# Causal attention ahead of a mixture of experts: diagonal half blocks of the scores and values as 64x64 matmuls, loads issued from the scores

## The chip, the core and the metric

The kernel runs on one core of one Trainium2 chip. The metric is the device time of one execution in microseconds (us), taken as the median of several runs. In the profile, PE is TensorE (PEld its weight loads), DVE is VectorE, ACT is ScalarE, POOL is GpSimd and SP is SyncE, which issues most of the DMA transfers. A line number such as L904 is a line of the kernel file of that profile.

## The reference

Eight sequences of 576 tokens, eight heads of 64 dimensions, everything in float32. Causal attention is computed with a per-head decay, and its output is the input of a mixture of eight experts in which every token goes to one expert, its own choice or that of the token before it.

```python
scores = scale * np.matmul(q, k.transpose(0, 1, 3, 2))
causal = np.triu(np.ones((S, S), dtype=bool), k=1)
cum = np.cumsum(np.maximum(s, 0.0), axis=-1)
bias = -(cum[:, :, :, None] - cum[:, :, None, :])
scores = np.where(causal, -1000000000.0, scores + np.minimum(bias, 0.0))
...
attn = attn / (np.sum(attn, axis=-1, keepdims=True) + 1e-09)
x = np.matmul(attn, v)                       # then (B, S, H * D)
...
e = fresh_e if s == 0 or local_gate[b, s] < 0.5 else prev_e
h = np.maximum(x[b, s] @ w1[e], 0.0)
out[b, s] = p[e] * (h @ w2[e])
```

## The kernel before

The kernel has two stages that follow each other on TensorE: attention, which also routes the tokens and stores them by expert in a table in HBM, and the experts, which fetch the table's rows and multiply them with the experts' weights (lines L608 and L637). The change lies in the attention stage.

Attention works on "pairs": two heads of one sequence, whose 64 dimensions each fill the two halves of the 128 partitions. There are 32 pairs (`NPAIR`), and the main loop (L1002) takes two of them in each of 16 rounds; a round is called a slot here. The 576 queries are nine blocks of 64 (`NJ`), the keys four chunks of 128 and a last chunk that holds the last 64 keys.

Scores are computed with keys on the output's partitions. `UNITS` says which key chunks and query ranges make one unit: (chunk, first query, last query, place). Four units make a pair, of 384, 384, 448 and 384 columns for each head (`WIDTH`). For a unit, `scores` (L893) takes a PSUM tile of two banks from the rotating pool `ps_s` of three such tiles, runs the matmuls of both heads (64 rows by 128 columns of the array each, the two heads on different rows), lets ScalarE write the exponential into a tile e (L905), and lets GpSimd set to zero what lies past the diagonal (`masked`, L890). A unit can start when the exponential of the unit three before it has emptied its tile. In a chunk that lies on the diagonal, an even query block needs only the first 64 of the 128 keys; the other 64 are computed and then masked.

Values follow when both pairs' eight units are issued: `values` (L924) multiplies, for each query block and each key chunk up to the diagonal, the exponentials (as weights, 128 rows by 64 columns, the two heads side by side) with the values vg, 66 columns wide: 64 dimensions, the key's decay weight, which sums to the denominator, and a one. A pair has 25 block-and-chunk steps for each head. The results lie in two tiles of the pool `ps_o` (blocks 0 to 5 and 6 to 8, `NJA`), each there once, so the second pair's values wait for the first's to be read. VectorE takes the reciprocal and multiplies into the token tile xb (L941, L942).

The values vg come from `weigh` (L876), which multiplies the loaded va with the keys' decay weights on VectorE; `WEIGHED` says up to which pair that is done at the end of each slot. Queries, keys and values come by DMA from SP, in order. A load is held back by a one-element ScalarE copy into its tile (L797, L808) that reads what the load shall follow: the second unit's exponential of the slot's second pair for values of six pairs ahead, and the first pair's outputs for queries and keys of four pairs ahead.

Each engine works in the order in which the program states its instructions[...]. Routing steps are hung into that order with `plan(slot, place, ...)`: places 0 and 1 are behind the first and second pair's scores, 3 and 4 behind their values, 5 at the slot's end. Three slots carry the routing's logits (lp, 160 columns on four 32-column parts of the array, from tiles of `ps_s`), three others the ranks (pos), and the last slot half a logits product; from the seventh slot on GpSimd stores rows of the table (L349).

Of the kernel before, what the change touches and what calls it, by code (L numbers as in the profile page):

```python
# [9 lines left out]
F32 = mybir.dt.float32  # L10
# [26 lines left out]
NJA = 6  # L37
G1 = 2
REF = (127, 415)
UNITS = (((0, 0, 384, 0),), ((0, 384, S, 0), (3, 384, S, 192)), ((1, P, S, 0),), ((2, 256, S, 0), (NF, TS, S, 320)))  # L40
WIDTH = (384, 384, 448, 384)
# [10 lines left out]
FIRST = ((0, P, 0, 3 * P), (P, S, 3 * P, S))  # L52
# [63 lines left out]
class Router:  # L116
# [104 lines left out]
    def logits(self, g, bs=range(GB)):  # L221
        v = self.nc.vector
        st = self.g[g]
        n, groups = self.columns(bs)
        lt = self.s("lt", [P, NJH, 2, WR])
        v.transpose(lt[:, :n].rearrange("p j q e -> p (j q e)"), st.pop("lp"))
        if "l" not in st:
            st["l"] = self.s("l", [P, NC, E + 1])
        l = st["l"]
        for c, (b, j, skip) in enumerate(groups):  # L230
            for r in range(2):
                v.tensor_copy(l[32 * r : 32 * r + 32, b * NJ + j + skip : b * NJ + j + n],
                              lt[32 * c : 32 * c + 32, skip:n, r, : E + 1])
        c = slice(bs[0] * NJ, bs[-1] * NJ + NJ)
        v.tensor_copy(l[DH:, c], l[:DH, c])
# [530 lines left out]
def attention(ctx, tc, q, k, v, s, wx, ident, recs, wend, router, experts):  # L766
# [10 lines left out]
    p_e = pool("p_e", 2)  # L777
    p_x = experts.p_x
# [8 lines left out]
    ins, vs, es, xs, xts = {}, {}, {}, {}, {}  # L787
    heads = [slice(DH * h, DH * h + DH) for h in range(2)]

    def load_qk(n, behind=None):  # L790

        if n >= NPAIR:
            return
        b, hp = divmod(n, HP)
        ins[n] = qb, kb = p_in.tile([P, S], F32, name="qb"), p_in.tile([P, S], F32, name="kb")
        if behind is not None:
            nc.scalar.copy(kb[0:1, 0:1], behind)  # L797
        for k0, k1, q0, q1 in FIRST if n == 0 else ((0, S, 0, S),):
            nc.sync.dma_start(kb[:, k0:k1], k[b][:, hp, k0:k1])  # L799
            nc.sync.dma_start(qb[:, q0:q1], q[b][:, hp, q0:q1])  # L800
# [23 lines left out]
    load_qk(2)  # L824
    load_v(2)
    load_qk(3)
    for n in range(3, NVA):
        load_v(n)
    router.projection(wx)
    wk = once.tile([P, NPAIR, G1 + NB, 2], F32, name="wk")  # L830
    nc.gpsimd.memset(wk[:TL, :, G1 + NF], 0.0)
    for t in vgs:
        nc.gpsimd.memset(t[..., VW - 1 : VW], 1.0)
        nc.gpsimd.memset(t[:TL, G1 + NF, :, VW - 1 : VW], 0.0)
# [19 lines left out]
    def key_weights():  # L854
        cps = banks("cps")[:, 0].rearrange("p (i n) -> p i n", n=B * H)
        i = 0
        for w, n in ((w1, G1), (w2, NB)):
            for c in range(n):
                a = min(c * P, S - P)
                tr(cps[:, i], w[:, a : a + P], ident[: B * H, : B * H])  # L860
                i += 1
        for i in range(G1 + NB):
            d = slice(TL if i == G1 + NF else 0, P)
            nc.vector.tensor_copy(wk[d, :, i, :].rearrange("p n h -> p h n"), cps[d, i].rearrange("p (h n) -> p h n", h=2))
# [24 lines left out]
    def masked(ap, n, base=0):  # L889
        nc.gpsimd.affine_select(out=ap, in_=ap, compare_op=Alu.is_ge, fill=0.0, base=base, pattern=n,  # L890
                                channel_multiplier=-1)

    def scores(n, u):  # L893
        if n >= NPAIR:
            return
        qb, kb = ins[n]
        if u == 0:
            es[n] = [p_e.tile([P, 2, w], F32, name=f"e{i}") for i, w in enumerate(WIDTH)]
        e = es[n][u]
        ps = banks("ps")[:, :, : WIDTH[u]]  # L900
        for c, a, z, at in UNITS[u]:
            key = min(c * P, S - P)
            for h, d in enumerate(heads):
                mm(ps[:, h, at : at + z - a], lhsT=kb[d, key : key + P], rhs=qb[d, a:z], start=True, stop=True)  # L904
        nc.scalar.activation(e, ps, Act.Exp, scale=scale)  # L905
        for c, a, z, at in UNITS[u]:
            m = min(P, z - a)
            if a < c * P + P:
                masked(e[:, :, at : at + m], [[0, 2], [1, m]], P - m)
# [14 lines left out]
    def values(n, j0, j1):  # L924
        b, hp = divmod(n, HP)
        if b not in xs:
            xs[b] = x_tile(b) if b < BX else p_x.tile([P, NJ, 2, XW], F32, name="xb")
        xb = xs[b]
        po = ps_o.tile([P, j1 - j0, VW], F32, name=f"po{j0}")
        for j in range(j0, j1):  # L930
            last = j // 2 if j < NJ - 1 else NF
            for c in range(last + 1):
                for h, d in enumerate(heads):
                    mm(po[d, j - j0, :], lhsT=weights_of(n, c, j, h),  # L934
                       rhs=vgs[n % NV][:, c if j < 2 * G1 else G1 + c, h, :],
                       start=(c == 0), stop=(c == last))

        def evacuate():
            m = j1 - j0
            rec = recs[:, n, j0:j1, :]  # L940
            nc.vector.reciprocal(rec, po[:, :, VW - 2 : VW])  # L941
            nc.vector.tensor_tensor(xb[:, j0:j1, :, 32 * hp : 32 * hp + 32], po[:, :, :DH].rearrange("p j (g i) -> p j g i", g=2),  # L942
                                    rec[:, :, 0].unsqueeze(2).unsqueeze(3).to_broadcast([P, m, 2, 32]), op=Alu.mult)

        return evacuate, po[0:1, 0, 0:1]
# [21 lines left out]
    for g in range(NG - 1):  # L967
        m = HP * GB // 2 * (g + 1)
        plan(m, 1, lambda g=g: router.product(g, of(g), banks))
        plan(m, 3, lambda g=g: router.logits(g))  # L970
        plan(m, 5, lambda g=g: (router.codes(g), router.turn1(g)))
        plan(m + 1, 1, lambda g=g: router.exps(g))
        plan(m + 1, 3, lambda g=g: router.turn2(g))
        plan(m + 2, 1, lambda g=g: router.ranks(g, banks))
        plan(m + 2, 3, lambda g=g: router.rows(g))
        plan(m + 2, 3, lambda g=g: router.gates(g, [xs[b] for b in range(g * GB, g * GB + GB)]))
# [13 lines left out]
    plan(m - 5, 3, lambda: router.assign_early(0))  # L990
# [5 lines left out]
    plan(m - 1, 3, lambda: router.logits(NG - 1, (0,)))  # L996
# [4 lines left out]

    for m in range(NPAIR // 2):  # L1002
        pair = 2 * m, 2 * m + 1
        for n in pair:
            for u in range(len(UNITS)):
                if (n, u) == (0, 2):
                    key_exps()
                scores(n, u)
                if (n, u) == (0, 3):
                    key_weights()  # L1010
                    weigh(0)
                    weigh(1)
                if (n % 2, u) == (1, 1):
                    load_v(n - 1 + NVA, es[n][u][0:1, 0, 0:1])
                    load_v(n + NVA)
            at(m, n - 2 * m)
        for n in pair:
            values(n, 0, NJA)[0]()
            evacuate, done = values(n, NJA, NJ)
            if n % 2 == 0:  # L1020
                load_qk(n + NV, done)
                load_qk(n + 1 + NV)
            evacuate()
            at(m, 3 + n - 2 * m)
# [44 lines left out]
def attention_general(ctx, tc, q, k, v, s, w_gate, w_local, cum_d, x_d, ident, lg):  # L1069
# [24 lines left out]
    def load_batch(b):  # L1094
# [7 lines left out]
        nc.sync.dma_start(kb, k[b])  # L1102
        for hp in range(HP):
            hs = slice(2 * hp, 2 * hp + 2)
            nc.sync.dma_start(vb[:, :, hs], v[b, hp][:, :NF])
            nc.sync.dma_start(vl[:, hs], v[b, hp][TL:, NF])
# [501 lines left out]
```

## Time and profile before

| | |
|---|---|
| Median of 3 runs | 729.83 us (729.41 to 730.94) |
| The profiled execution | 748.85 us, of which the span of its instructions 747.1 us |
| Mean granted TensorE clock in it | 0.994 of full speed |
| PE busy | 729.2 us, 98% of the span, 6537 records |
| PEld, DVE, ACT, POOL busy | 504.9, 257.7, 166.0, 206.7 us |
| Value matmuls (L934) | 3200 records, 105.2 us |
| Score matmuls (L904) | 768 records, 94.7 us |
| Exponentials (L905) | 128, 97.0 us |
| Masks (L890) | 160, 67.2 us |
| HBM traffic | 249 GB/s over the span |

The busy time of an engine is the union of its records. A float32 matmul of the kernel leaves two matmul records, one for each of its two passes, and as many weight loads; two matmuls on different parts of the array run at the same time, so the mean duration of a record says little, and a stage's length is read from the chain of waits or from the order in time. The records of the first expert matmul start 221.6 us into the span; what lies before that is the attention stage.

### The profile page before, as it was taken

To read this page: it belongs to the slowest core of one execution; us is meant where nothing else is said; L and a number is where in the kernel's file an instruction comes from. 1 tells how busy PE (TensorE), PEld (TensorE's weight loads), DVE (VectorE), ACT (ScalarE), POOL (GpSimd) and SP (SyncE) were. 2 spreads that over 40 slices of the span, in tenths; PEclk is the share of its full clock that TensorE was granted. 3 is DMA by queue.
4 is the path that set the end of the run, shared out by engine and by line. 5 is a ranking of instruction groups with operands and counts; after the bars stand their busy time and mean duration, and the time that the engine had idled before them with its cause. 6 is when DMAs were issued, how large, how long until landed. Compare 5 with 4: busy or idle time off the path is not lost.

```text
span 747.1 us, 16231 instructions
## 1 busy us (share of the span) xinstructions
PE 729.2 (98%) x6537; PEld 504.9 (68%) x6537; DVE 257.7 (34%) x714; ACT 166.0 (22%) x355; POOL 206.7 (28%) x453
## 2 busy tenths in 40 slices
PE   8999999999998999999999999999999999999996
PEld 7888878878876567567567365637644676673675
DVE  4656668677756383101100411041132001104110
ACT  4645454354331011011011010201010111110111
POOL 3543367577574245350100011010101001000100
PEclk9999999999998999999999999999999999999999
DMA  8464455665629996598555979996999965976700
GB/s 303 145 189 149 152 191 165 201 199 172 188 81 382 341 396 218 208 424 240 203 190 169 375 258 396 342 382 237 425 334 390 423 215 214 307 268 239 269 15 32
DMA packets 57205, 187.28 MB, mean 251 GB/s; under 512 B 11837, under 2 KB 32061, under 8 KB 49568
## 3 DMA queue, kind: packets, MB, share of 16 engines
q1 hardware_dynamic: 50224, 165.91, 62.3%
q0 software_dynamic: 6800, 20.09, 7.0%
q8 instruction: 53, 0.87, 0.5%
q14 instruction: 32, 0.26, 0.1%
q10 hardware_dynamic: 96, 0.15, 0.1%
HBM read 165.50 MB, written 20.75 MB: 249 GB/s over the span
## 4 chain that ended last, share of the span: by engine, by line
PE 95%; issue 2%; POOL 1%; DVE 1%; DMA 1%; ACT 0%; SPq 0%; POOLq 0%; ACTq 0%
PE yp L637 34%; PE hp L608 31%; PE po L934 13%; PE ps L904 11%; PE hp L599 4%; PE lp L217 2%; DMA qb<-in_q_dram 1%; POOL table L349 0%; ACT e L905 0%; PE pos L301 0%; POOL e L890 0%; PE pos L302 0%; DVE xb L942 0%; SPq L799 0%; POOL out_dram L641 0%
## 5 line engine op out<-in xcount | busy, mean ns | idle before, releaser
L637 PE MATMUL yp<-w2b,hT 128*128 128x512 f32 (+4 forms) x768 | 258.4, 584 | 0.0
L608 PE MATMUL hp<-xT,w1b 128*128 128x256 f32 (+2 forms) x1216 | 232.0, 352 | 0.0
L608 PEld LDWEIGHTS hp<-xT,w1b 128*128 128x128 f32 x1216 | 207.7, 192 | 30.0 <-issue 7.8
L637 PEld LDWEIGHTS yp<-w2b,hT 128*128 128x128 f32 (+3 forms) x768 | 109.9, 167 | 138.4 <-issue 136.1
L641 POOL DMA_INDIRECT out_dram<-y,gi x37 | 36.4, 984 | 412.3 <-DVE y L639 380.0
L610 ACT ACTIVATE hT<-hp 128x256 f32<-128x256 f32 (+2 forms) x152 | 53.6, 353 | 430.4 <-PE hp L608 417.2
L639 DVE TENSOR_SCALAR y<-yp,gi 128x512 f32<-128x512 f32 (+2 forms) x38 | 27.8, 731 | 299.8 <-PE yp L637 293.4
L934 PE MATMUL po<-vg,e 128*64 128x66 f32 x3200 | 105.2, 223 | 6.9 <-issue 5.6
L934 PEld LDWEIGHTS po<-vg,e 128*64 128x64 f32 x3200 | 98.7, 138 | 13.1 <-issue 10.5
L905 ACT ACTIVATE e<-ps 128x768 f32<-128x768 f32 (+1 forms) x128 | 97.0, 837 | 46.5 <-PE ps L904 45.8
L904 PE MATMUL ps<-qb,kb 64*128 64x192 f32 (+4 forms) x768 | 94.7, 398 | 0.6 <-ACT e L905 0.3
L904 PEld LDWEIGHTS ps<-qb,kb 64*128 64x128 f32 x768 | 64.7, 186 | 29.6 <-ACT e L905 14.9
L890 POOL TENSOR_SCALAR_AFFINE_SELECT e<-e 128x256 f32<-128x256 f32 (+1 forms) x160 | 67.2, 444 | 50.3 <-ACT e L905 49.3
L349 POOL DMA_INDIRECT table<-xb,idx x54 | 54.5, 1009 | 19.6 <-issue 16.8
L619 DVE STREAM_TRANSPOSE hT<-hs 32x256 f32<-32x256 f32 x64 | 27.9, 436 | 78.9 <-ACT hs L601 78.1
L884 DVE TENSOR_TENSOR vg<-va,wk 128x256 f32<-128x256 f32 x64 | 41.5, 714 | 0.0
L941 DVE RECIPROCAL recs<-po 128x12 f32<-128x12 f32 x64 | 13.5, 211 | 64.0 <-PE po L934 45.2
L599 PE MATMUL hp<-w1b,xT 128*32 128x512 f32 (+1 forms) x224 | 28.3, 594 | 0.0
L578 DVE STREAM_TRANSPOSE xT<-xq 128x1024 f32<-128x1024 f32 (+1 forms) x23 | 23.6, 1028 | 11.8 <-DMA xq<-table 11.7
L942 DVE TENSOR_TENSOR xb<-po,recs 128x384 f32<-128x384 f32 (+1 forms) x48 | 22.0, 458 | 2.2 <-POOL xb L325 0.6
L599 PEld LDWEIGHTS hp<-w1b,xT 128*32 128x32 f32 (+1 forms) x224 | 8.1, 114 | 17.8 <-issue 17.8
L953 DVE STREAM_TRANSPOSE xt<-xb 128x576 f32<-128x576 f32 x24 | 17.1, 751 | 0.0
(254 smaller groups left out, 202.6 us busy)
## 6 DMA issues: line engine op xcount, KB each, us to landing
w2b<-in_w_dram SPq DMA_DIRECT2D x30, 2048.0 KB
w1b<-in_w_dram SPq DMA_DIRECT2D x29, 2048.0 KB
va<-in_v_dram SPq DMA_DIRECT2D x32, 320.0 KB
kb<-in_k_dram SPq DMA_DIRECT2D x31, 288.0 KB
qb<-in_q_dram SPq DMA_DIRECT2D x31, 288.0 KB
xq<-table SPq DMA_DIRECT2D x56, 130.0 KB
w1b<-in_w_dram SPq DMA_DIRECT2D x4, 512.0 KB
xq<-table SPq DMA_DIRECT2D x20, 65.0 KB
```

The lines of the kernel that those rows point to most:

```text
L349: put = self.nc.gpsimd.indirect_dma_start(out=self.halves, in_=src, element_offset=0, in_offset=None, out_offset=bass.IndirectOffsetOnAxis ...
L599: mm(ps[d, :], lhsT=xT[:, k, d], rhs=self.ws[l][0][:, k, c * 512 : c * 512 + 512], start=(k == 0), stop=(k == DK - 1))
L608: mm(ps[:, :w], lhsT=self.ws[ls[0]][0][:, k, c * P : c * P + P], rhs=xT[:, k, :w], start=(k == 0), stop=(k == DK - 1))
L610: nc.scalar.activation(self.hT[u][:, c, :w], ps[:, :w], Act.Relu)
L619: self.nc.vector.transpose(hT[32 * a : 32 * a + 32, :, 32 * r : 32 * r + 32], hs[32 * r : 32 * r + 32].rearrange("p (c i) -> p c i", i=P)[ ...
L637: mm(ps[d, :], lhsT=hT[:, k, n * P + d.start : n * P + d.stop], rhs=self.ws[l][1][:, k, f : f + w], start=(k == 0), stop=(k == FK - 1))
L641: put = nc.gpsimd.indirect_dma_start(out=self.out[:, :], out_offset=bass.IndirectOffsetOnAxis(ap=gi.bitcast(I32)[:m, n, 0:1], axis=0), in_ ...
L884: nc.vector.tensor_tensor(vg[:, to].rearrange("p c h e -> p (c h) e")[:, :, :DH], va[:, :c].rearrange("p c h e -> p (c h) e"), wk[:, n, to ...
L890: nc.gpsimd.affine_select(out=ap, in_=ap, compare_op=Alu.is_ge, fill=0.0, base=base, pattern=n, channel_multiplier=-1)
L904: mm(ps[:, h, at : at + z - a], lhsT=kb[d, key : key + P], rhs=qb[d, a:z], start=True, stop=True)
L905: nc.scalar.activation(e, ps, Act.Exp, scale=scale)
L934: mm(po[d, j - j0, :], lhsT=weights_of(n, c, j, h), rhs=vgs[n % NV][:, c if j < 2 * G1 else G1 + c, h, :], start=(c == 0), stop=(c == last))
```

## The change

The nine key blocks are stored in another order (`BLOCKS`: 8, 0, 1, 2, 3, 5, 4, 7, 6), so that four chunks of 128 keys hold blocks 0 and 1, 2 and 3, 5 and 4, 7 and 6, and block 8 stands alone in front. The host orders the keys and values so. A unit then contains only whole chunks: for each chunk, the queries from its second block on. Three units make a pair, of 512, 448 and 384 columns. What is left, query blocks 0, 4, 2 and 6 with their own 64 keys, is computed apart: `scores_halves` does this for both pairs of the next slot in 16 matmuls of 64 rows, 64 columns and 64 moving columns, with one exponential and two masks for both pairs; `values_halves` multiplies them with the values, 8 matmuls of 64 rows by 64 columns for each pair. Whole values take 21 steps for each head.

The order of a slot becomes: six score units, half values of the first pair, half scores of the next slot, half values of the second pair, whole values of the first, whole values of the second. The second pair's outputs (pb) lie in a tile of the rotating pool `ps_s` that the score units use too; the first pair's stay in `ps_o`. Output parts are blocks 0 to 3 and 4 to 8.

Loads are held back by the slot's own first exponentials: values of four and five pairs ahead by the first unit of the first pair, queries and keys of four pairs ahead by the third unit of the first pair and the second unit of the second pair, each with its one-element copy. The logits' copies go from VectorE to ScalarE where both sequences are there, and several routing steps move from place 3 to place 1.

```diff
-NJA = 6
+NJA = 4
...
-UNITS = (((0, 0, 384, 0),), ((0, 384, S, 0), (3, 384, S, 192)), ((1, P, S, 0),), ((2, 256, S, 0), (NF, TS, S, 320)))
-WIDTH = (384, 384, 448, 384)
+BLOCKS = (8, 0, 1, 2, 3, 5, 4, 7, 6)
+UNITS = (((0, DH, S, 0),), ((1, 3 * DH, S, DH), (NF, TS, S, 0)), ((2, 5 * DH, S, 0), (3, 7 * DH, S, 256)))
+WIDTH = (512, 448, 384)
...
+HALVES = ((0, 4), (2, 6))
...
-        for k0, k1, q0, q1 in FIRST if n == 0 else ((0, S, 0, S),):
-            nc.sync.dma_start(kb[:, k0:k1], k[b][:, hp, k0:k1])
-            nc.sync.dma_start(qb[:, q0:q1], q[b][:, hp, q0:q1])
+        todo = [(kb, k, 0, S), (qb, q, 0, S)] if n else [(kb, k, 0, DH + P), (qb, q, 0, FIRST), (qb, q, FIRST, S), (kb, k, DH + P, S)]
+        for to, src, a, z in todo:
+            nc.sync.dma_start(to[:, a:z], src[b][:, hp, a:z])
...
-        for c, a, z, at in UNITS[u]:
-            m = min(P, z - a)
-            if a < c * P + P:
-                masked(e[:, :, at : at + m], [[0, 2], [1, m]], P - m)
+        if u == 0:
+            masked(e[:, :, :DH], [[0, 2], [1, DH]], DH)
+        elif u == 1:
+            masked(e[:, :, :P], [[0, 2], [1, P]])
+        else:
+            masked(e[:DH].rearrange("p h (t i) -> p (h t) i", t=2)[:, :, :DH], [[0, 4], [1, DH]])
+
+    def scores_halves(m, ps):
+        if 2 * m >= NPAIR:
+            return
+        eh[m] = p_eh.tile([P, 2, 2, len(HALVES), DH], F32, name="eh")
+        ps = ps[:, :, : 4 * DH]
+        for i in range(2):
+            qb, kb = ins[2 * m + i]
+            for t, blocks in enumerate(HALVES):
+                for side, x in zip(heads, blocks):
+                    at = (2 * i + t) * DH
+                    key = BLOCKS.index(x) * DH
+                    for h, d in enumerate(heads):
+                        mm(ps[side, h, at : at + DH], lhsT=kb[d, key : key + DH], rhs=qb[d, x * DH : x * DH + DH],
+                           start=True, stop=True)
+        nc.scalar.activation(eh[m].rearrange("p h n t i -> p h (n t i)"), ps, Act.Exp, scale=scale)
+        by = eh[m].rearrange("p h n t i -> p (h n t) i")
+        masked(by[:DH], [[0, 8], [1, DH]])
+        masked(by, [[0, 8], [1, DH]], DH)
...
+    def room(n):
+        if n % 2:
+            po = banks("pb")
+            po = [po[:, i] for i in range(2)]
+        else:
+            po = [ps_o.tile([P, 512], F32, name=f"po{i}") for i in range(2)]
...
+    def values_halves(n, po, first):
+        e = eh[n // 2][:, :, n % 2]
+        for t, blocks in enumerate(HALVES):
+            for part, (side, j) in enumerate(zip(heads, blocks)):
+                for h, d in enumerate(heads):
+                    mm(po[part][d, j - PARTS[part][0], :], lhsT=e[side, h, t],
+                       rhs=vgs[n % NV][side, j // 2 + (G1 if part else 0), h, :],
+                       start=(first > 0 and t == 0), stop=(first == 0 and t == 1))
...
-        plan(m, 3, lambda g=g: router.logits(g))
+        plan(m, 1, lambda g=g: router.logits(g))
...
-        plan(m + 1, 3, lambda g=g: router.turn2(g))
+        plan(m + 1, 1, lambda g=g: router.turn2(g))
...
-        plan(m + 2, 3, lambda g=g: router.rows(g))
-        plan(m + 2, 3, lambda g=g: router.gates(g, [xs[b] for b in range(g * GB, g * GB + GB)]))
+        plan(m + 2, 1, lambda g=g: router.rows(g))
+        plan(m + 2, 1, lambda g=g: router.gates(g, [xs[b] for b in range(g * GB, g * GB + GB)]))
...
+    def loads(n, u):
+        step = n % 2, u
+        if (n, u) == (2, 1):
+            load_v(n + NV, es[n][u][0:1, 0, P : P + 1])
+            load_v(n + 1 + NV)
+        elif step == (0, 0):
+            n = n if n > 2 else 0
+            load_v(n + NV, es[n or 2][u][0:1, 0, DH : DH + 1])
+            load_v(n + 1 + NV)
+        elif step == (0, 2):
+            load_qk(n + NV, es[n][u][0:1, 0, DH : DH + 1])
+        elif step == (1, 1):
+            load_qk(n + NV, es[n][u][0:1, 0, P : P + 1])
...
                 scores(n, u)
...
-                if (n % 2, u) == (1, 1):
-                    load_v(n - 1 + NVA, es[n][u][0:1, 0, 0:1])
-                    load_v(n + NVA)
+                if n > 1:
+                    loads(n, u)
             at(m, n - 2 * m)
-        for n in pair:
-            values(n, 0, NJA)[0]()
-            evacuate, done = values(n, NJA, NJ)
-            if n % 2 == 0:
-                load_qk(n + NV, done)
-                load_qk(n + 1 + NV)
-            evacuate()
-            at(m, 3 + n - 2 * m)
+        a, b = pair
+        po = room(a)
...
+        values_halves(a, po, m)
+        halves = banks("ph") if b + 1 < NPAIR else None
+        to = room(b)
+        scores_halves(m + 1, halves)
+        values_halves(b, to, True)
...
+        for i in range(2):
+            if m:
+                values(a, po, i, False, True)
+            evacuate(a, po, i)
+        at(m, 3)
+        for i in range(2):
+            values(b, to, i, False, True)
+            evacuate(b, to, i)
+        at(m, 4)
```

## The prediction

> **What bounds the kernel now.** The page's chain of waits, by engine and line, comes first; then the chain in order of time for two ordinary slots of the attention stage (a slot is one pass of the loop over two head pairs):
>
> ```profile
> PE 95%; issue 2%; POOL 1%; DVE 1%; DMA 1%; ACT 0%; SPq 0%; POOLq 0%; ACTq 0%
> PE yp L637 34%; PE hp L608 31%; PE po L934 13%; PE ps L904 11%; PE hp L599 4%; PE lp L217 2%; DMA qb<-in_q_dram 1%; POOL table L349 0%; ACT e L905 0%; PE pos L301 0%; POOL e L890 0%; PE pos L302 0%; DVE xb L942 0%; SPq L799 0%; POOL out_dram L641 0%
> ```
>
> ```profile
> 55.39 5.76 PE ps L904 x48
> 61.15 2.31 PE lp L217 x64
> 63.46 5.98 PE po L934 x200
> 69.44 5.76 PE ps L904 x48
> 75.20 5.98 PE po L934 x200
> ```
>
> TensorE carries it; the change touches only the attention lines (ps, po). An ordinary slot is 5.76 us of scores and 5.98 us of values, 11.74 us, with no wait of TensorE in the chain. There are 16 slots; three also hold lp (2.31 us), three the two pos matmuls (0.72 us), the last a half lp (1.46 us).
>
> The third view is ScalarE inside one score stage, in order of time. Columns: start, length, engine and line, count.
>
> ```profile
> 71.10 1.61 ACT L905 ACTIVATE e<-ps 128x768 f32<-128x768 f32 x2
> 72.61 1.51 ACT L905 ACTIVATE e<-ps 128x768 f32<-128x768 f32 x2
> 73.30 1.53 ACT L905 ACTIVATE e<-ps 128x768 f32<-128x768 f32 x2
> 74.86 0.19 ACT L808 COPY va<-e 1x1 f32<-1x1 f32 x1
> 74.95 1.59 ACT L905 ACTIVATE e<-ps 128x896 f32<-128x896 f32 x2
> ```
>
> Same trace, narrower windows: exponentials start at 70.39, 71.10, 71.80, 72.61, 73.30, 73.99, 74.95, 75.76. Back to back, one of 768 elements occupies ScalarE 0.69 to 0.71 us and one of 896 0.81 us (71.80 to 72.61), although it finishes 0.1 us later than that. Around the one-element copy the step is 74.95 - 73.99 = 0.96 us: the copy reads the tile just written, so ScalarE runs empty, and it costs 0.28 us (0.27 by these roundings). TensorE ends its unit 0.27 us before the exponential starts (70.12, 70.39). ScalarE is thus almost as full as TensorE here, yet its fifth exponential (73.30) still frees its bank in time.
>
> **The profiled run against the others.** It took 748.85 us (span 747.1), the median is 729.83. The last nine slots, from 93.65 to 221.63 in the chain, took 128.0 us, where clean ones would take 9 x 11.74 + 2 x 2.31 + 1.46 + 2 x 0.72 = 113.2: TensorE shows gaps marked "issue" there. The half lp behind them spans 226.94 to 232.69, 5.75 us instead of 1.46, and the clock granted between 228 and 240 us is 0.72, some 3 us more. Together about 22 us, as much as the difference. So I take the timed runs' slots as clean (11.74 us), cost the change against those, and move the median by the same amount.
>
> **Per-pass prices, same score stage.** A matmul record is one of two passes. 448 columns: 70.77 to 71.15, 0.375 us; four of 192: 0.65 us; so 0.84 ns a column: 512 columns 0.43, 256 0.216, 128 0.109, 64 0.056 us. Two heads' records run at once on two parts of the array. Values: 0.0583 us a pass (5.98/100, less the switch). Leaving scores for values costs 75.13 against 74.93 + 0.06, and a first pass 0.05 longer: 0.20 us; values to scores the same (0.10 before, 0.10 in the first pass).
>
> **The skill.** "TensorEngine Tiling (Array Packing)", Key Properties, says that changing the tiling mode drains TensorE and that tiles run independently; the two 0.20 us switches agree with the first. For the second, lp has four column tiles: 64 records of 160 columns are sixteen groups of 0.134 us, 2.15 us, and 2.31 is measured. A 64x64 mode no run here shows. "TensorE: Matmul & The Clock Gate", LDWEIGHTS, prices a weight load by its columns over 1.2 GHz: 53 ns for 64, just inside a 56 ns pass; agreeing, a 128-column load behind a 64-column pass delays the next by 0.056 us. Its section on measured packing reports sixteen row-and-column tiles at 10.6 times; I lean on that.
>
> **The change, part by part (ordinary slot).**
> *Scores.* Per pair 1,600 columns become 512 + 384 + 64 + 256 + 128 = 1,344: two passes each are 0.86 + 0.644 + 0.112 + 0.432 + 0.218 = 2.27 us against 2.70. Two pairs 4.54, plus 0.11 behind the 64-column passes, plus 0.10 first pass: 4.75.
> *Half scores.* 16 matmuls on four quadrants: 4 groups x 2 passes x 0.056 = 0.45 us. Pairwise it would be 0.90.
> *Half values.* 8 per pair on four quadrants: 4 passes x 0.058 = 0.23 us for each pair.
> *Whole values.* 21 instead of 25 key chunks per pair: 84 passes x 0.0583 = 4.90 against 5.83.
> *Switches.* Three modes a slot instead of two: 0.20 more (bounds 0 and 0.25; I take 0.20, as both present ones).
> TensorE alone: 4.75 + 0.20 + 0.23 + 0.45 + 0.23 + 0.20 + 4.90 + 0.10 = 11.06 us, 0.68 less than now.
> *Banks.* The second pair's outputs leave ps_o and take the three rotating score banks. Counting allocations, half scores take the bank of the fourth exponential, pb that of the fifth; the third unit of the next slot takes pb's, freed about 1 us into that slot by two VectorE reads (0.2 + 0.5 us), needed at 1.8: hidden, with 0.8 us to spare.
> *Loads.* The slot's three copies now sit inside the chain of exponentials: behind the first, third and fifth. The transfers behind them wait on SP for the copy, and are needed a slot later, 12 us or more: hidden. The copies are not. Behind each stand the remaining exponentials, and behind those pb.
> Chain to pb: first exponential 0.96 + 0.27 = 1.23; 1,024 elements 0.92 (768 and 896 extrapolated); copy 0.28; 896 at 0.81; 768 at 0.70; copy 0.28; 0.92; 0.81; finish 0.10: 6.05 us. The current trace restarts a weight load 0.05 us after an exponential ends; with the load, 0.15: pb at 6.2. TensorE gets there at 5.6 (5.8 with a short wait for the second exponential before). Then 0.23 + 0.20 + 4.90 + 0.10: 11.63 us. So 0.57 of the 0.68 us is handed back, and a slot gains 0.11.
> *Masks and the rest.* Five selections a pair (0.3 to 0.4 us each) become three, plus two wide ones for the halves, which are read a slot later: hidden, and values start later than now. Logit copies move from VectorE to ScalarE in three slots, behind the exponentials, ahead of only the half exponential: hidden. Moving rows, gates and turns to an earlier place puts up to 3.5 us of VectorE work ahead of the first pair's evacuation; po is wanted 5 us into the next slot: hidden. Start: first transfers differ by 32 KB.
>
> **The sum.** Eight ordinary slots x -0.11 = -0.9. Three lp slots: lp takes the fourth bank at 5.4 (a 0.25 us wait) and then hides the rest: about 13.9 against 14.06, -0.5 together. Three pos slots shift pb to the sixth exponential, behind the third copy, 7.1: about 12.53 against 12.46, +0.2. Last slot, no half scores: -0.6. First slot, less scoring but two more switches and key weights as now: -0.7 (0 to -1.5). Together -2.5: 727.3 us.
>
> **Rivals.**
> *Full gain.* If the copies cost nothing in the chain, pb is free at 5.64, as TensorE arrives: fifteen slots x -0.68 and the first, -10.5: 719.3. For it: TensorE is 95% of the chain. Against: the measured 0.28 us. It decides once the chain is 0.57 us shorter.
> *Slower: quadrants run two by two.* Halves cost 0.47 + 0.90 + 0.47 instead of 0.91. TensorE reaches pb at 6.5, past ScalarE; the slot is 12.2, +0.45 x 8; lp slots +0.76, pos slots +0.7; about +8.5 in all: 738. For it: no 64x64 record in the trace. Against: lp. It decides where the 1.8 us of halves exceeds about 1.4, the saving less the switch.
> *Starved halves.* 128 instructions (64 records and as many weight loads) in 0.91 us is 140 a us; the densest stretch shown is half lp, 128 in 1.46. At that rate a slot loses 0.17 on top: 730, no change.
>
> **Chances.** Main case 0.52 (own range 725 to 729.5); full gain 0.15; between them, if the new switch is free or the copies overlap partly, 0.06; starved 0.15; two by two 0.12. Faster or slower counts beyond 0.2% (1.5 us), about what a measurement of this kernel can tell from no change. Faster: 0.40 of the main case + 0.15 + 0.05 = 0.60; same: 0.10 + 0.07 = 0.17; slower: the rest, 0.23. For 8 in 10 the range reaches the full gain and part of the slow side: 719 to 734.
>
> **What would show it.** Right: about 11.6 us a slot; a wait of weight loads before the second pair's half values, on an exponential, of about 0.4 us; steps over 1.1 us from a 1,024-element exponential across a copy; 64-column half scores in groups of four within 0.06 us. Wrong: no such wait and slots near 11.1 (full gain); half scores near 0.9 us (pairs); waits on masks or transfers inside a slot; new gaps in the experts' stage, which I hold unchanged.

## The result and the profile after

The changed kernel takes **739.2 us** (median of 6 runs, 733.23 to 742.35), the kernel before 730.41 (729.41 to 731.36) beside it: a ratio of 1.0108 with a 95% interval of 1.0067 to 1.0149, slower where 727.3 was forecast. The profiled execution took 739.1 us, its span is 737.4; the trace below is of this one execution, while the six runs spread over 9 us and those of the kernel before over 2.

The page of the changed kernel, its DMA queues (packets, MB, share of 16 engines) and the chain by engine and line:

```profile
q1 hardware_dynamic: 50224, 165.91, 63.7%
...
q8 instruction: 56, 0.92, 0.5%
...
PE 94%; issue 1%; ACT 1%; DMA 1%; POOL 1%; SPq 0%; DVE 0%; POOLq 0%; ACTq 0%
PE yp L642 35%; PE hp L613 31%; PE ps L915 10%; PE pb L974 6%; PE po L974 5%; PE hp L604 4%; PE lp L221 1%; DMA va<-in_v_dram 1%; ACT e L916 1%; PE ph L937 1%; PE pb L986 1%; PE po L986 1%; SPq L806 0%; POOL table L354 0%; DVE wk L871 0%
```

TensorE still carries it. What went wrong shows only slot by slot, in the chain in order of time of the changed kernel: a clean slot from 32.96 to 44.38, and the next.

```profile
32.96 5.07 PE ps L915 x40
38.03 0.39 PE po L986 x16
38.42 0.47 PE ph L937 x32
38.89 0.44 PE pb L986 x16
39.33 2.60 PE po L974 x84
41.93 2.45 PE pb L974 x84
44.38 5.07 PE ps L915 x40
49.45 0.39 PE po L986 x16
49.84 0.47 PE ph L937 x32
50.30 0.44 PE pb L986 x16
50.74 2.60 PE po L974 x84
53.34 1.33 PE pb L974 x45
54.68 1.69 issue
56.37 1.38 PE pb L974 x39
```

The clean slot is 11.42 us; it was 11.74 before. The second loses 1.85 us in the middle of its last matmuls (from the last matmul's due start to 56.37), and the profile names no engine and no transfer as the releaser: "issue". Such a gap stands in nine further places behind it, and one of 0.8 us ahead of it, at 32.63.

**What the gaps have in common.** I numbered TensorE's records in order of start: its 13,850 weight loads and matmuls and the 117 records of its sequencer, most of them semaphores, between them. The first instruction behind each long gap of this trace has number 192 or 193 above a multiple of 256: 2,241 at 56.37, 4,033 at 95.87, 4,545 at 109.09, 6,336 at 149.75, 6,849 at 163.63. (Without the sequencer's records the pattern is lost: the remainders are then 169, 157, 151, 137 and 131.) Queue q8 of the page carries 56 packets of 16 KB, and TensorE starts about 256 instructions from one packet to the next: I read them as its program, as its 13,967 records make 54.6 packets of 256. Mostly a packet comes 180 to 295 instructions after the last. Ahead of these five gaps it is 384 to 453, and nowhere else in the trace over 376; the packet that is missing at 54.68 moves at 53.99, the one before it at 43.94. At a distance of 256 to 290 instructions it would have moved at 51.1 to 51.6 us, so it is 2.4 to 2.9 us late. I conclude that TensorE has run to the end of its packet and waits for the next one.

The windows of the same trace (us, busy time of TensorE, its weight loads, VectorE, ScalarE, GpSimd; granted clock; DMA share; GB/s) show what the packet competes with, and what a long gap costs besides:

```profile
50.00:52.00 2.00, 2.00 (x82) 1.82 (x74) 0.56 (x2) 1.60 (x4) 1.13 (x3) 1.00 0.96 291
52.00:54.00 2.00, 2.00 (x76) 2.00 (x74) 0.65 (x3) 0.22 (x1) 1.01 (x2) 1.00 1.05 394
54.00:56.00 2.00, 0.68 (x23) 0.54 (x19) 0.68 (x3) 0.00 (x0) 0.00 (x0) 1.00 0.49 184
...
109.00:110.00 1.00, 0.91 (x26) 0.91 (x28) 0.00 (x0) 0.00 (x0) 0.52 (x1) 0.84 0.16 58
110.00:111.00 1.00, 1.00 (x24) 1.00 (x22) 0.00 (x0) 0.00 (x0) 0.00 (x0) 0.50 0.47 150
111.00:112.00 1.00, 1.00 (x16) 0.88 (x14) 0.22 (x1) 0.22 (x1) 0.00 (x0) 0.50 0.03 4
```

From 50 to 54 us the 16 engines are full with the slot's loads, and the packet starts in the burst's last microsecond. After the gaps of 2.28 us (109.09) and 2.88 us (163.63) the granted clock is 0.50 for about 3.4 us each, 1.7 us lost each. "TensorE: Matmul & The Clock Gate", Part 1, names an idle window of about 3.4 us for that; here 2.3 us of idling came before it.

**Two levels of chips.** The runs fell on several chips. The kernel before takes 730 us on some (as in both comparisons above) and 746 on others; the profile of before, at 748.85 us, is of the second kind. Each numbered chip served one group of runs, so that the level belongs to the chip and not to the time of the runs is not shown; "chip of the 746 level" below means no more than what the kernel before took there. Ratios are always against the kernel before on the same chip. For each trace two sums are given: gaps of over 0.2 us between the starts of consecutive matmuls, beyond the first one's two passes, from 40 us to the end of attention (which leaves out a late packet near 32 us that several of the traces have), (a) at a packet's end, numbers 192 and 193, and (b) within 3 us behind the start of a GpSimd table store. The changed kernel's trace above has (a) 11.1 and (b) 0.4; before's has 0.2 and 10.3.

### The profile page after: what moved, and what is told of

It is laid out like the page before. It is cut to its first block, busy times and chain, and to the rows that moved or that the text cites. A ratio compares the mean times of both kernels' runs of the same rounds, so it can differ in the third digit from the quotient of the medians.

```text
span 737.4 us, 16944 instructions
## 1 busy us (share of the span) xinstructions
PE 717.6 (97%) x6925; PEld 493.2 (67%) x6925; DVE 251.4 (34%) x689; ACT 168.5 (23%) x381; POOL 202.7 (27%) x421
## 4 chain that ended last, share of the span: by engine, by line
PE 94%; issue 1%; ACT 1%; DMA 1%; POOL 1%; SPq 0%; DVE 0%; POOLq 0%; ACTq 0%
PE yp L642 35%; PE hp L613 31%; PE ps L915 10%; PE pb L974 6%; PE po L974 5%; PE hp L604 4%; PE lp L221 1%; DMA va<-in_v_dram 1%; ACT e L916 1%; PE ph L937 1%; PE pb L986 1%; PE po L986 1%; SPq L806 0%; POOL table L354 0%; DVE wk L871 0%
## 5 line engine op out<-in xcount | busy, mean ns | idle before, releaser
L916 ACT ACTIVATE e<-ps 128x1024 f32<-128x1024 f32 (+2 forms) x96 | 83.3, 905 | 60.1 <-PE ps L915 55.8
L915 PE MATMUL ps<-qb,kb 64*128 64x64 f32 (+5 forms) x644 | 84.8, 415 | 0.8 <-ACT e L916 0.8
L915 PEld LDWEIGHTS ps<-qb,kb 64*128 64x128 f32 x644 | 53.3, 191 | 30.5 <-ACT e L916 11.2
L899 POOL TENSOR_SCALAR_AFFINE_SELECT e<-e 128x128 f32<-128x128 f32 (+2 forms) x96 | 41.5, 441 | 54.3 <-ACT e L916 53.6
L974 PE MATMUL pb<-vg,e 128*64 128x66 f32 x1344 | 46.7, 228 | 9.8 <-issue 7.5
L974 PEld LDWEIGHTS pb<-vg,e 128*64 128x64 f32 x1344 | 43.9, 143 | 11.2 <-issue 8.8
L974 PE MATMUL po<-vg,e 128*64 128x66 f32 x1344 | 43.2, 223 | 0.3 <-issue 0.3
L974 PEld LDWEIGHTS po<-vg,e 128*64 128x64 f32 x1344 | 40.8, 138 | 1.6 <-issue 0.4
L892 DVE TENSOR_TENSOR vg<-va,wk 128x256 f32<-128x256 f32 x64 | 37.4, 647 | 0.0
L583 DVE STREAM_TRANSPOSE xT<-xq 128x1024 f32<-128x1024 f32 (+1 forms) x23 | 23.6, 1027 | 14.3 <-DMA xq<-table 14.1
L899 POOL TENSOR_SCALAR_AFFINE_SELECT eh<-eh 64x512 f32<-64x512 f32 (+1 forms) x32 | 21.1, 660 | 12.4 <-ACT eh L939 8.9
## 6 DMA issues: line engine op xcount, KB each, us to landing
w2b<-in_w_dram SPq DMA_DIRECT2D x30, 2048.0 KB, 12.5
```

The costliest lines, as they stand in the source:

```text
L892: nc.vector.tensor_tensor(vg[:, to].rearrange("p c h e -> p (c h) e")[:, :, :DH], va[:, :c].rearrange("p c h e -> p (c h) e"), wk[:, n, to ...
L916: nc.scalar.activation(e[:, :, : WIDTH[u]], ps, Act.Exp, scale=scale)
L974: of = mm(po[part][d, j - a, :], lhsT=weights_of(n, c, j, h), rhs=vgs[n % NV][:, c if j < 2 * G1 else G1 + c, h, :], start=(first and i == ...
```

## The experiments

### Where the loads stand

Both kernels with the other's loads, and the changed kernel with half of the loads moved back (chip of the 746 level, before 745.82 us).

`e1_old_loads`: the changed kernel, all loads at before's places.

```diff
-        step = n % 2, u
-        if (n, u) == (2, 1):
...
-        elif step == (0, 2):
-            load_qk(n + NV, es[n][u][0:1, 0, DH : DH + 1])
-        elif step == (1, 1):
-            load_qk(n + NV, es[n][u][0:1, 0, P : P + 1])
+        if (n % 2, u) == (1, 1):
+            load_v(n - 1 + NVA, es[n][u][0:1, 0, P : P + 1])
+            load_v(n + NVA)
...
+            if i:
+                load_qk(a + NV, po[1][0:1, 0, 0:1])
+                load_qk(b + NV)
             evacuate(a, po, i)
```

> The changed kernel with its loads at the places of the kernel before (values six pairs ahead behind the second unit of the second pair, queries and keys behind the first pair's outputs); all matmuls as changed. Theory (TensorE's instruction fetch comes late behind the load transfers, which the change puts under the instruction-rich half and whole values): the issue gaps of 0.5 to 2.9 us in pb vanish or nearly, a slot takes 11.2 us, and the time is 720 to 725 us. Rival A (more instructions, 544 instead of 496 a slot and 128 of them within 1 us, starve TensorE wherever the loads stand): gaps as before, 734 to 740 us. Rival B (the copies within ScalarE's chain cost the time): only 0.2 us a slot, so 3 us less than the changed kernel.

747.71 us, ratio 1.0017 (1.0005 to 1.0029), a miss: 720 to 725 would have been 0.986 to 0.993 of the kernel before. Clean slots of 11.11 us are as expected and most late packets are gone, (a) 2.7; but (b) is 13.9.

`e1_before_new_loads`: the kernel before with `loads` as in the change, behind its own units.

```diff
-                if (n % 2, u) == (1, 1):
-                    load_v(n - 1 + NVA, es[n][u][0:1, 0, 0:1])
-                    load_v(n + NVA)
+                if n > 1:
+                    loads(n, u)
...
-            if n % 2 == 0:
-                load_qk(n + NV, done)
-                load_qk(n + 1 + NV)
```

> The kernel before with its loads let go as the change does it (values behind the first unit of the first pair, queries and keys behind the last unit of the first pair and the third of the second); all matmuls as before. Theory (late instruction fetch): issue gaps of about 1 us in several slots, 735 to 745 us. Rival A (the denser instruction stream): no new gaps, 730 to 733 us, the copies in the chain of exponentials alone adding up to 0.2 us a slot.

748.86 us, 1.0039 (1.0023 to 1.0056). Score stages of 6.14 instead of 5.76 us: the copies in the chain of exponentials cost 0.38 us a slot. (a) 0.5, (b) 9.7: with before's matmuls the loads' new place makes hardly a packet late. The gaps of about 1 us in several slots that the theory expected here did not come, so a burst of loads alone is not enough either.

`e1_old_qk`: the changed kernel, only queries and keys at the old place.

```diff
-        elif step == (0, 2):
-            load_qk(n + NV, es[n][u][0:1, 0, DH : DH + 1])
-        elif step == (1, 1):
-            load_qk(n + NV, es[n][u][0:1, 0, P : P + 1])
...
+            if i:
+                load_qk(a + NV, po[1][0:1, 0, 0:1])
+                load_qk(b + NV)
             evacuate(a, po, i)
```

> The changed kernel with only the loads of queries and keys at the place of the kernel before; values' loads as changed. Theory: these four transfers of a slot (1.15 MB) make most of the burst under the values, so most of the loss goes: 722 to 728 us. Rival A: 734 to 740 us.

744.35 us, **0.9974** (0.9959 to 0.9989): faster than before by 0.26%, at the edge of what was expected (722 to 728 would have been 0.989 to 0.997). Clean slots of 11.21 us, (a) 0.6, (b) 15.7.

`e1_old_v`: only the values' loads at the old place, so that all of a slot's loads come closely behind each other.

```diff
...
-        elif step == (0, 2):
+        if step == (1, 1):
+            load_v(n - 1 + NVA, es[n][u][0:1, 0, P : P + 1])
+            load_v(n + NVA)
+        if m and step == (0, 2):
             load_qk(n + NV, es[n][u][0:1, 0, DH : DH + 1])
...
```

> The changed kernel with only the loads of values at the place of the kernel before (six pairs ahead, second pair's second unit); queries and keys as changed. Theory: now all transfers of a slot are let go within 2 us and fall under the values; gaps stay or grow: 736 to 745 us. Rival A: 734 to 740 us. It tells little between these two, but much against the other three runs.

753.8 us, 1.0082 (1.0045 to 1.0119); (a) 8.1, (b) 13.4. So the place of queries and keys makes the long gaps, and a longer burst makes them longer. But (b) was new: gaps in all four kernels that have nothing to do with packets. In `e1_old_qk`, GpSimd and TensorE in order of time:

```profile
100.61 1.00 POOL L354 DMA_INDIRECT table<-w1b,idx  x1 [0.16 <-issue]
101.62 0.18 POOL L353 COPY gap<-recs 1x1 f32<-1x1 f32 x1
101.95 0.98 POOL L354 DMA_INDIRECT table<-w1b,idx  x1 [0.16 <-issue]
```

```profile
100.80 1.43 PE L974 MATMUL pb<-vg,e 128*64 128x66 f32 x30
102.63 0.34 PE L974 MATMUL pb<-vg,e 128*64 128x66 f32 x4 [0.40 <-issue]
103.37 0.46 PE L974 MATMUL pb<-vg,e 128*64 128x66 f32 x7 [0.40 <-issue]
```

The first matmul behind a first gap starts about 1.3 us after the store's start (1.2 to 1.35 us in four traces); behind two stores there are three gaps of 0.3, 0.55 and 0.55 us, four to ten instructions apart, at any number modulo 256. Stores that fall on scores, with few instructions a us, are followed by hardly any.

### The same on one chip, with the changed kernel beside them

Chip of the 746 level, before 746.59 us. `e2_after` is the changed kernel, `e2_old_qk` is `e1_old_qk`, `e2_before` the kernel before for its trace. `e2_half_qk` moves only the second pair's queries and keys back:

```diff
-        elif step == (1, 1):
-            load_qk(n + NV, es[n][u][0:1, 0, P : P + 1])
...
+            if i:
+                load_qk(b + NV, po[1][0:1, 0, 0:1])
             evacuate(a, po, i)
```

> The changed kernel itself, on the same chip as its variants. Theory 'late fetch': TensorE's instructions come in packets of 256, and a packet asked for behind a burst of loads comes late; the program order number of the first matmul after each long gap is then 192 or 193 above a multiple of 256, in 5 to 8 slots, 8 to 13 us in all. Theory 'stores': what costs the time are GpSimd's stores of table rows that fall on dense matmuls, 0.4 to 0.7 us each; gaps then begin 1.2 to 1.4 us after a store's start, three behind two stores. On a chip where the kernel before takes 746 us both would add up to about 753; where it takes 730, 738 to 740 with late fetches, and gaps at stores would be absent in both kernels, if they are what sets that chip apart.

> The changed kernel with queries and keys loaded where the kernel before does it (behind the first pair's whole values), the values' loads as in the change. Late fetch: no gap at a packet's end, packets never more than about 310 instructions apart; 0.8 to 1.4% less than the changed kernel on this chip, and 0.2 to 0.9% less than the kernel before. Density (128 instructions of the halves in 1 us run TensorE's sequencer dry, whatever the loads do): the same time as the changed kernel within 0.3%.

> The changed kernel with the first pair's queries and keys loaded at the change's place, and only the second pair's at the old place, so that the burst is half as long. Late fetch behind the burst: at least half of the long gaps at packets' ends go, 0.4 to 1.2% less than the changed kernel. If instead the one-element copies between the exponentials did the harm, one of three is out of the chain: 0.1 to 0.3 us a slot, 0.2 to 0.6%, with the gaps as in the changed kernel.

> The kernel before, for its trace on this chip. If gaps at table stores are what sets its two levels apart: at about 730 us no such gaps, slots of 11.74 us throughout, last value matmul at about 209 us and an experts' stage of 520 us; at about 746, 10 to 12 us of gaps at stores, the last value matmul at about 221 and 524 to 526 us of experts' stage. If the levels come from elsewhere (a slower clock, a slower DMA), slots without gaps differ between them.

| | us | ratio (interval) | (a) | (b) |
|---|---|---|---|---|
| e2_before | 746.33 (one run) | | 0.6 | 9.3 |
| e2_after | 751.85 | 1.0075 (1.0051 to 1.0098) | 6.6 | 12.9 |
| e2_half_qk | 746.51 | 1.0009 (0.9998 to 1.0020) | 4.3 | 12.5 |
| e2_old_qk | 743.28 | 0.9962 (0.9952 to 0.9972) | 0.5 | 14.7 |

Undoing the place of the queries and keys takes 8.6 us off; undoing half of it, 5.3. Late packets account for 6.1 of the 8.6, the 0.2 us of a clean slot for most of the rest. Of the half undoing's 5.3 they account for 2.3 only: of the packets' gaps over 0.2 us five of seven stay, where at least half of the long ones were expected to go. Density alone (the rival in which the halves run the sequencer dry whatever the loads do) is refuted: `e2_old_qk` has the same matmuls. Where the burst falls in `e2_old_qk` shows in its windows (columns as above): on the end of the values and then on scores, with 31 and 22 matmuls in 2 us instead of 76.

```profile
76.00:78.00 2.00, 2.00 (x76) 2.00 (x72) 1.86 (x8) 0.37 (x3) 0.00 (x0) 1.00 0.27 62
78.00:80.00 2.00, 2.00 (x31) 1.33 (x28) 1.67 (x5) 0.17 (x1) 0.00 (x0) 1.00 0.98 347
80.00:82.00 2.00, 2.00 (x22) 1.15 (x18) 2.00 (x4) 1.97 (x4) 0.85 (x2) 1.00 0.51 189
```

Density holds for (b) instead: the same stores cost the changed matmuls 12.5 to 14.7 us, before's 9.3. Most of the level of 746 thus goes with stores: the two traces of before have 9.3 and 10.3 us of (b) in attention, and in their half lp 2.9 and 3.3 us of gaps behind stores, with 3.4 and 6.8 us at half clock at their end; the first trace of the changed kernel has 0.4 and neither of the others. The 753 expected of `e2_after` was 1 us high: its packets were less late than on the first chip.

### The stores moved onto the scores

One edit to three kernels; a number is the place in a slot, 5 its end.

```diff
-STORES = (((5,), (0, 1, 3, 4, 5), (0, 1, 3, 4, 5), (0, 1, 3, 4, 5), (0, 0)), ((5, 5), (0, 1, 3, 4, 5), (0, 1, 3, 4, 5), (0, 1, 1, 3, 4, 5)),
-          ((5, 5), (0, 0, 1, 1, 3, 4, 5, 5)))
+STORES = (((5, 5, 5, 5), (5, 5, 5, 5), (5, 5, 5, 5), (5, 5, 5, 5), (5, 5)), ((5, 5), (0, 5, 5, 5, 5), (0, 5, 5, 5, 5), (0, 1, 5, 5, 5, 5)),
+          ((5, 5, 5, 5), (0, 1, 5, 5, 5, 5)))
```

> The kernel before with the same table stores, but most of them four in a row at the end of a slot, so that they fall on the next slot's scores, where none of the stores so far was followed by a gap. Theory 'stores': gaps behind stores fall from about 10 us to 3 to 5, the time by 5 to 7 us (ratio 0.991 to 0.994) on a chip of the 746 us level, and by nothing on one of 730. Rival: the gaps belong to the density of the value matmuls and merely coincide with stores; the gaps stay and so does the time, within 0.2%. The masks stand behind the stores on GpSimd; if that costs, the first pair's whole values wait for a mask.

> The changed kernel with the same edit of the stores. Stores: gaps behind stores fall from about 14 us to about 5, the time from 1.0075 to 0.993 to 0.997 of the kernel before on a chip of the 746 us level. The gaps at packets' ends (7 of them, about 7 us) stay, since the loads stay: late fetches are another cause. If both were one cause, they go too, and the ratio comes under 0.988.

> The changed kernel with queries and keys loaded at the old place and the stores moved: neither late fetches nor most of the gaps at stores. What is left is the change's own gain of 0.5 us a slot, 8 us in 16 slots, against the kernel before with its stores moved too; against the kernel before as it is 0.980 to 0.986, about 733. If the halves' density costs by itself, it stays above 0.99.

This time the chip was of the 730 level (before 730.08), where stores should cost nothing wherever they are.

| | us | ratio (interval) | (a) | end of attention, us into the span |
|---|---|---|---|---|
| e3_before_stores | 750.15 | 1.0273 (1.0242 to 1.0303) | 0.2 | 229.0 |
| e3_after_stores | 740.9 | 1.0141 (1.0107 to 1.0174) | 14.2 | 218.7 |
| e3_old_qk_stores | **722.22** | **0.9889** (0.9873 to 0.9906) | 1.7 | 202.5 |

The changed kernel stays where it was, with 11 late packets; the third row differs from it only in the place of the queries' and keys' loads, takes 18.7 us less, and is 1.1% faster than the kernel before. Its chain over one ordinary slot, 11.21 us:

```profile
68.83 5.07 PE ps L915 x40
73.90 0.39 PE po L986 x16
74.29 0.47 PE ph L937 x32
74.75 0.23 PE pb L986 x16
74.99 2.60 PE po L974 x84
77.59 2.45 PE pb L974 x84
```

Sixteen slots of 0.53 us less are 8.5 us; 7.9 are measured. The changed kernel with its stores in place and only these loads moved back was not run on a chip of this level. The kernel before lost 20 us, more than any case of the expectation: the waits for masks that it names as possible came to 17 us of gaps. Its chain:

```profile
100.22 0.98 POOL table L349
101.20 0.01 issue
101.21 0.43 POOL e L890
101.64 0.04 issue
101.69 7.39 PE po L934 x200
```

Four stores hold GpSimd for 5 us, the masks come behind them, and values that follow directly on the scores wait for the masks. The changed order has 1.1 us of half work in between and three masks for a pair instead of five: one such wait, of 1.26 us, in the whole of `e3_old_qk_stores`.

### Copies or transfers, and the stores on the other level

`e4_copies`: `e2_old_qk` with the change's two one-element copies, into a scratch tile and with no load behind them. `e4_dummy`: with three reads of 262 KB behind them, into tiles that nobody uses.

```diff
+        elif step in ((0, 2), (1, 1)):
+            at_ = DH if u == 2 else P
+            nc.scalar.copy(gate[0:1, 0:1], es[n][u][0:1, 0, at_ : at_ + 1])
```

```diff
-NVA = 6
+NVA = 4
...
+        elif step in ((0, 2), (1, 1)) and n + NV < NPAIR:
+            at_ = DH if u == 2 else P
+            b, hp = divmod(n + NV, HP)
+            to = dummy[:2] if u == 2 else dummy[2:]
+            nc.scalar.copy(to[0][0:1, 0:1], es[n][u][0:1, 0, at_ : at_ + 1])
+            for t, src in zip(to, (k, q)):
+                nc.sync.dma_start(t, src[b][:, hp, :512])
```

> Queries and keys loaded at the old place, but two one-element copies stand between the exponentials where the change has them, into a scratch tile and without a transfer behind them. If the transfers make the packets late: no gap of over 1 us at a packet's end; an ordinary slot of 11.42 instead of 11.21 us, since the fifth exponential frees the bank 0.2 us late, so 2 to 3 us, 0.3 to 0.4%, over the same kernel without the copies. If the copies or their place make the gaps: the time of the changed kernel, about 8 us more.

> The same with transfers behind the two copies: three reads of 262 KB a slot into scratch tiles that nobody uses (two thirds of the bytes of the change's loads there), while the real loads stay at the old place. The copies for the loads of values and their four instead of six tiles are no part of the question. If the transfers make the packets late: gaps at packets' ends come back (matmul number 192 or 193 over a multiple of 256), 4 to 10 us in all, 0.5 to 1.3% over the kernel with copies alone. If not the bytes but the position of the real loads counts: as the kernel with copies alone.

> The changed kernel with queries and keys loaded at the old place and nothing else. On a chip of the 730 us level: 722 to 724, 0.989 to 0.992, as much as with the stores moved, since stores cost nothing there. On one of 746: 0.996 to 0.997, as twice before.

> The same with the table's stores moved onto the scores. On a chip of the 730 us level 0.989 as before. On one of 746, if gaps behind stores are a cost of their own: 5 to 10 us less than with the stores in their old places, 0.982 to 0.990. If the stores merely coincide with gaps: within 0.2% of it.

Chip of the 746 level, before 745.72.

| | us | ratio (interval) | (a) | (b) |
|---|---|---|---|---|
| e4_old_qk | 744.11 | 0.9970 (0.9959 to 0.9982) | 0.5 | 14.8 |
| e4_copies | 746.83 | 1.0009 (0.9996 to 1.0022) | 0.0 | 15.4 |
| e4_dummy | 752.85 | 1.0094 (1.0059 to 1.0130) | 4.4 | 14.1 |
| e4_old_qk_stores | 740.77 | 0.9925 (0.9901 to 0.9948) | 1.5 | 9.1 |

The copies alone cost 2.7 us, 0.17 a slot, and make no packet late: a clean slot of `e4_copies` is 11.41 us (43.02 to 54.43). `e4_dummy` costs 6.0 on top, although nobody waits for the data of its reads. Not all of that is theirs: its second edit, four tiles for values instead of six, makes two of the values' copies on ScalarE wait for VectorE's weighing, 2.3 us together, which `e4_copies` does not show. The late packets, 4.4 us, are the part that comes with the reads. From the chain of `e4_dummy`, at instruction 2,753, again 193 above a multiple of 256:

```profile
64.27 1.54 PE po L974 x47
65.81 1.20 issue
67.01 1.27 PE po L974 x37
```

So transfers behind the copies make packets late, and the copies do not. As for the stores, moving them takes 3.3 us off on this level, 5.7 of (b): gaps behind stores are a cost of their own and go with the stores, but I had expected 5 to 10. A fourth store in a row still falls on the halves, where TensorE's instructions are densest (0.5 us each), and others on lp.

**What stays open.** Why stores cost nothing on one chip and 0.3 to 0.6 us each on another. How a packet is asked for and why it stands behind loads: "DMA: Bandwidth & Descriptors", Queues, rings and completion order, says that an engine goes round its queues packet by packet, by which I would not expect 2.4 us of delay and more; the traces show only that it occurs. And `e1_old_loads` has cleaner slots than `e1_old_qk` but takes 3.4 us more. In their traces it has 2.1 us more of late packets, and its experts' stage is 1.5 us longer (526.1 against 524.6), with the clock at half for 6.8 us instead of 3.4; why the clock differs there stays open.

## Why the prediction was wrong, point by point

**What failed: "Loads ... hidden".** The step asked who needs the loaded data and when. It should also have asked what else the burst delays. The loads' new place puts four reads of queries and keys, behind values, into the slot's densest 4 us: 128 instructions in 1.1 us of halves and then 69 a us of whole values. TensorE then needs a packet every 3.5 us, and the packet comes behind the loads. The cost of that, put at nothing, was 11.1 us, and 3.4 us more at half clock. The forecast had named new gaps as a sign of being wrong, but in the experts' stage, and they came in attention; the experts' stage is unchanged as said (519.7 us behind the last value matmul, 519.5 to 519.6 in the three kernels with moved stores).

**The sum, with what it measured.** All from the changed kernel's chain, against the prediction's clean 11.74, 14.05 (with lp), 12.46 (pos), 13.20 (last):

| | forecast, us | measured, us |
|---|---|---|
| eight ordinary slots | -0.9 | -2.6 (11.42) |
| three lp slots | -0.5 | -1.3 (13.63, from 57.75 to 71.38) |
| three pos slots | +0.2 | -0.6 (12.44, 12.44 and 11.93 without their late packets) |
| last slot | -0.6 | -1.1 (12.10) |
| first slot | -0.7 | +0.5 (ends 20.38, before 19.85) |
| late packets behind 40 us | 0 | +11.1 |
| half clock behind two of them | 0 | +3.4 |
| together | -2.5 | +9.4 |

+8.8 is the difference of the medians. The work on TensorE was forecast too pessimistically by 2.6 us, and two terms were missing. The first slot had only been guessed. That the sum comes so near is partly luck: clean slots leave out 1.9 us that the changed kernel's trace has, the late packet at 32.63 and smaller waits, and by the medians the kernel before must have some 2.6 us beside its clean slots too, of which no trace at the 730 level was taken.

**The bank wait: right mechanism, half the size.** 0.57 us was forecast in front of the second pair's halves; the chain has 0.44 for matmuls that take 0.23 where nothing delays them, a wait of 0.21. The chain of exponentials was nearly right: in the second slot shown the fifth ends at 50.23 and the first half-value matmul behind it starts at 50.28, 5.97 us behind the slot's first score matmul (44.31), where 6.2 was forecast. TensorE arrived some 0.2 us later than the forecast 5.6, because the scores are 5.07 us and not 4.75 (4.96 in `e1_old_loads`, without the copies). Undone in `e1_old_loads`, the wait is gone, and the slot is 11.11; "TensorE alone: 11.06" was right.

**Halves and switches: right.** po L986 0.39 with its switch (forecast 0.43), ph 0.47 (0.45), pb L986 0.23 (0.23), whole values 5.05 with switch and first pass (5.20). Four quadrants do run at once; "two by two" is refuted.

**Rivals.** "Full gain" needed a chain 0.57 us shorter; the version without copies behind queries and keys shows it (11.21), and 722.22 us is near its 719.3 (its own terms, fifteen times 0.68 and 0.7, give 10.9 and 718.9). "Two by two" has with 738 the time nearest to the result, by luck: its mechanism did not occur. "Starved halves" had the resource right, TensorE's supply of instructions, and place, cause and size wrong: halves ran at full rate, and the shortage came a packet later, through the loads. It gave 0.17 us a slot where up to 2.9 were lost in one. No rival joined the two changes, denser instructions and a burst at the same place, though each stood in the text.

**The profiled run against the others.** I took its 22 us of gaps for an accident of that execution. They recur at that level in the kernel before: (b) is 9.3 and 10.3 us in its two traces. Costing clean slots was right all the same, as the comparison was made on a chip without those gaps; on the other kind the change is slower too, by 0.75%.

## What to carry to other kernels

When work on TensorE becomes denser, count instructions a microsecond as well as passes, and ask where the next packet of its program comes from at that moment: a burst of loads whose data nobody needs for 12 us can stop TensorE for 3 us, and the profile only says "issue". If a gap marked so recurs, number the instructions, the sequencer's too; here the gaps that stood always at the same place in 256 were the program arriving late, and what helped was to let the loads run later, from the slot's last matmuls into the next slot's scores, which have many columns and few instructions. And cost a load's new place by who shares the DMA engines with it, not only by when its data is used.

## What the runs showed of the hardware that was not expected

- TensorE's program comes in 16 KB packets of about 256 instructions, which the page counts on the same 16 DMA engines as the loads; with these full (DMA share 0.96 to 1.05), a packet came up to 200 instructions late and TensorE stood still for 0.2 to 2.9 us.
- Behind GpSimd's table stores dense matmuls stop for 0.3 to 0.6 us, and the first starts again about 1.3 us after a store's start, on the chips where the kernel before takes 746 us and not where it takes 730. Moving the stores took 5.7 of these 14.8 us away; why one chip has them and another not is open.
- In the attention stage every gap of TensorE of 2.3 us and more (2.28 and 2.88 in the changed kernel, 2.4 in `e1_old_v`, 3.0 and 3.1 in `e3_before_stores`) was followed by half the clock for 3.4 us. Of gaps from 1.7 to 2.2 us two were (1.7 and 1.9 in `e3_before_stores`) and others not (2.2 in `e3_after_stores`), so no threshold is shown.
- Matmuls of 64 rows by 64 columns run four at once: sixteen with 64 columns, two passes each, in 0.47 us with their part of the switch.
